# Decoding float64 weights: the sign bit by a narrowed copy on GpSimd or ScalarE, the second block's triangular solve on VectorE spread over the first block's Mish units, and the chain behind it moved beside the first expert

## The chip, the cores and the metric

One NeuronCore of one Trainium2 chip runs the whole kernel in one launch. The metric is the device time of the launch in microseconds (us). TensorE is called PE here, VectorE DVE, ScalarE ACT, GpSimd POOL, and the engine that issues the DMAs SP.

## The reference

A delta-rule attention feeds a dense layer with a Mish activation, which feeds a mixture of eight experts whose gates are balanced by eight Sinkhorn rounds. Cut to what is computed:

```python
for t in range(S):                      # q, k, v: [4, 8, 768, 48]
    y[:, :, t] = einsum(q_t, state)
    v_old = einsum(state, k_t)
    state = state + beta_t * outer(k_t, v_t - v_old)
x = y as [3072, 384]
h = x @ w_in                            # w_in [384, 2048]: float64
x = (h * tanh(softplus(h))) @ w_out     # w_out [2048, 384]: float64
P = exp(x @ w_gate), scaled eight times by rows and columns
out = sum over e of P[:, e] * (relu(x @ w1[e]) @ w2[e])   # 8 experts, 1024 wide
```

`w_in` and `w_out` come from numpy as float64, so the kernel gets their 64-bit words and has to make float32 values of them itself.

## The kernel before

The 768 positions are cut into six **blocks** (`c` = 0 to 5) of 128 positions, each with all 4 x 8 heads. For each block the delta rule needs the inverse of 32 x 32 triangles (the **solve**) and then a **chain** of small matrix products; its result, `x1`, is the input of the dense layer.

The solve: `lane_in_one` transposes `gx` into `lane`; `elim_ops` gives 60 operations (30 products into `t`, 30 sums into `lane`); `st_lane_out` transposes the result into `t` and `yd`; then `st_m1`, `st_place` and `st_m2` join the quarters with 128 and 128 matmuls of 32 x 32. The chain (`chain_list`) is z, w, s, y for two halves of the block, each stage a pair of tiles: matmuls into a bank called `psa`, and an eviction (`r`, `us`, `us`, `yd`). Block 0's solve and chain run in a **start** written out by hand.

After the start, `window(c)` places the work of the next block beside the matmuls of block c. Block 0 has 16 **Mish units** (marks s0 to s15), then marks f1 to f4, then 8 units of expert 0 (marks s16 to s23). A Mish unit f is: `m_first`, nine matmuls into `psh` (called gemm f below); Mish and a rounded copy `gh` on ACT; the rest `gl` on DVE (`m_c`); and `m_second`, nine matmuls into `x`. There are two `psh` banks, so gemm f+2 waits until `gl` f has read its bank. After the last unit, `x2_done` evicts `x`, which expert 0 reads. At the end of the block `st_x1` turns `yd` into the next block's `x1`. Blocks 2 to 5 have a Mish part of their own each, and only blocks 0 and 1 an expert part; a second phase with the other experts follows.

Each Mish unit of block 0 needs one **chunk** of 128 columns of `w_in` and 128 rows of `w_out`, made of 64-bit words in a tile of 128 x 1536 words of 32 bits (`bits`, `xr`, and from chunk 4 on four `kq` tiles in turn). Of each number the tile has a low and a high 32-bit word, so each operation works on 128 x 768 with a stride of two words. The decode is

- ACT (`begin_decode`): the high word, read as float32, times 2^-112, which moves the exponent's bias;
- DVE `tail`: low word shifted right by 29;
- DVE `shift`: low word = high word shifted left by 3, or low word;
- DVE `sign`: low word = sign bit of the high word, or low word;
- ACT rounds the float32 into a weight slot `w`, and DVE subtracts to get the rest (`convert`), after which SP fetches the chunk that reuses the tile.

Operations on an engine run in the order in which the program issues them, apart from what the framework moves up where nothing stands against it. Three queues set the order on DVE: `dq` holds decode steps, `eq` the solve's operations with a cost each, and `fill(us)` issues operations of `eq` at the end of a unit until their costs reach `us`. `PLACES[0]` says at which marks the next block's solve is finished (its first number), at which the sixteen chain stages stand (the list behind it), and from which mark on the solve after it is queued (its last number but one). In the list of marks 0 to 15 are s0 to s15, 16 to 19 are f1 to f4, and 20 to 27 are s16 to s23.

Of the kernel before, what the change touches and what calls it, by code (L numbers as in the profile page):

```python
# [10 lines left out]
F16 = mybir.dt.float16  # L11
I32 = mybir.dt.int32
AF = mybir.ActivationFunctionType
ALU = mybir.AluOpType
# [70 lines left out]
def delta_mish_sinkhorn_kernel(  # L85
# [94 lines left out]

    def queue_decode(i):

        if kind(i) != "wide":
            return
        b = bits(i).rearrange("p (n w) -> p n w", w=2)
        low, high = b[:, :, 0], b[:, :, 1]

        def tail():
            nc.vector.tensor_scalar(out=low, in0=low, scalar1=29, scalar2=None, op0=ALU.logical_shift_right)

        def shift():
            nc.vector.scalar_tensor_tensor(
                out=low, in0=high, scalar=3, in1=low, op0=ALU.logical_shift_left, op1=ALU.bitwise_or
            )

        def sign():
            nc.vector.scalar_tensor_tensor(
                out=low, in0=high, scalar=-0x80000000, in1=low, op0=ALU.bitwise_and, op1=ALU.bitwise_or
            )
            decoded[0] = i + 1  # L200

        dq.extend([(0.47, tail, i), (0.87, shift, i), (0.87, sign, i)])

    def begin_decode(i):
        high = bits(i).rearrange("p (n w) -> p n w", w=2)[:, :, 1].bitcast(F32)
        nc.scalar.activation(out=high, in_=high, func=AF.Copy, scale=2.0 ** -112)
        queue_decode(i)
        begun[0] = i + 1
# [28 lines left out]
    def flush_stores():  # L237

        while late_stores:
            late_stores.popleft()()  # L240

    def convert():
        i = ncvt[0]
        if kind(i) == "wide":
            while decoded[0] <= i:
                while not dq:
                    begin_decode(begun[0])
                dq.popleft()[1]()
        ncvt[0] += 1
        w = wslots[loads[i][2]]  # L250
        ch = loads[i][1]
        if kind(i) == "again":
            flush_stores()
            nc.sync.dma_start(out=w.bitcast(F32), in_=w_dram[ch])
            return
        if kind(i) == "wide":
            r = bits(i).rearrange("p (a b w) -> p a b w", a=2, w=2)[:, :, :, 0].bitcast(F32)
        else:
            r = raws.pop(i)
        nc.scalar.activation(out=w[:, 0], in_=r, func=AF.Copy)  # L260
# [516 lines left out]
    def o_store():  # L777

        u, half, t = todo.popleft()
        if t < 0:  # L780
            f, x, (n, d) = fin[u], slice(512 * half, 512 * half + 512), divmod(~t, KD)
            tt(out=f[:, d, x], in0=f[:, d, x], in1=f[:, 3 + 3 * n + d, x], op=ALU.add)
            return
            return True
        o_write(u, half, t, o_turn(u, half, t, (0, 1, 2)))
# [10 lines left out]
    if True:  # L796
# [277 lines left out]

        def elim_ops(c, eng=(nc.vector,)):
            ops = []
            for s in range(1, 31):
# [3 lines left out]
                def prod(s=s, n=n, slot=slot):  # L1081
                    slot[0] = t11.rearrange("p b i -> p (b i)")[:, 0:n * s].rearrange("p (n s) -> p n s", s=s)
                    eng[0].tensor_tensor(  # L1083
                        out=slot[0], in0=lane[:, s + 1:32, s:s + 1].to_broadcast([128, n, s]),
                        in1=lane[:, s:s + 1, 0:s].to_broadcast([128, n, s]), op=ALU.mult,
                    )

                def add(s=s, n=n, slot=slot):
                    eng[0].tensor_tensor(  # L1089
                        out=lane[:, s + 1:32, 0:s], in0=lane[:, s + 1:32, 0:s], in1=slot[0], op=ALU.add  # L1090
                    )
# [265 lines left out]
        with tc.manual_schedule():  # L1357
# [61 lines left out]
            for t in range(4):  # L1419
                run(*[lambda hf=hf: st_g(1, t, hf, False) for hf in range(2)])  # L1420
            for n in range(4):
                begin_decode(n)
# [9 lines left out]

            def elim1(n, eng):
                elim_eng[0] = eng
                for _ in range(min(n, len(ops1))):
                    ops1.popleft()[1]()

            m1a = m_run(st_m1(0, 0, (32,)))
            m1a[0]()
            st_place(0, 0, (0, 2))  # L1440
            dec(2)
            m1b, m2a = m_run(st_m1(0, 1, (32,)), st_m2(0, 0, (0,)))
# [9 lines left out]
            for p in wa:  # L1452
                p()
            dec(1)
            st_place(0, 1, (0, 1, 2, 3))
            m2b = m_run(st_m2(0, 1, (0,)))
            s0 = [st_s(0, t) for t in range(2)]
            m2b[0]()
            for t in range(2, 4):
                prep_v_act(0, t)  # L1460
            s0[0]()
            s0[1]()
            converts(1)
            z1 = [st_z(0, t) for t in range(2, 4)]
            z1[0]()
            gq[0]()
            z1[1]()
            gq[1]()
            run(*[lambda t=t: st_y(0, t) for t in range(2)])
            for n in range(4, 6):  # L1470
                fetch(n)
            for t in range(4):
                diag_left(1, t)
            in1 = [op for _, op in lane_in_one(1)]
            elim_eng = [nc.gpsimd]
            ops1 = deque(elim_ops(1, elim_eng))
            dec(2)
            wb = [st_w(0, t) for t in range(2, 4)]
# [5 lines left out]
            for n in range(6, 8):  # L1484
                fetch(n)
            decodes(2)
            converts(2)
            dec(2)
            x1h, x1l = [late_p.tile([128, KD, 512], F32R, tag=f"e{i}", name=f"x{i}") for i in range(2)]
# [7 lines left out]
            converts(3)  # L1497
            elim1(18, nc.gpsimd)
            decodes(4)
            converts(4)  # L1500
            elim_eng[0] = nc.vector
            wslots.append(late_p.tile([128, 2, 2, DM], F32R, tag="e2", name=f"w{NS1 - 1}"))
# [9 lines left out]
        def drain_decode():  # L1512
# [4 lines left out]
        PLACES = [  # L1517
            (11, two(14, 15, 17, 18, 19, 20, 21, 22), 16, [21, 22, 23, 24], two(23, 24, 25, 26), 18, 26, 26),
            (5, spread(8, 23, 1, 16), 1, [8, 9, 11, 13], spread(10, 19, 1, 8), 1, 27, 19),
# [4 lines left out]
        def window(c):  # L1524
# [53 lines left out]
        with tc.manual_schedule():  # L1578
            banks[:] = [0, [A1, A1]]
            for c in range(NBLK):  # L1580
# [36 lines left out]
                for f in range(U1 + (3 if c < NE0 else 2)):  # L1617
# [240 lines left out]
```

## Time and profile before

| what | value |
|---|---|
| median of 3 runs | 2230.39 us (2229.17 to 2235.85) |
| the profiled execution's own time | 2229.53 us |
| its span in the profile | 2227.7 us |
| PE busy, share of the span | 2165.4 us, 97% |
| DVE busy | 1394.4 us, 63% |
| ACT busy | 691.9 us, 31% |
| POOL busy | 673.6 us, 30% |

The span is what the trace covers; the profiled execution's time is 1.8 us more, and the median 0.9 us above that. A busy share is a mean over the whole span; the change touches the first 290 us of it, where the shares differ from the mean. The time at the start of an operation is counted from the span's start.

### The profile page before, as it was taken

The page shows a single profiled execution, that of the slowest core. Times are in us where ns is not written, and L with a number is a line of the kernel's source. Part 1 is how long each engine was busy: PE and PEld are TensorE (multiplying, and loading weights), DVE is VectorE, ACT ScalarE, POOL GpSimd, SP SyncE. Part 2 cuts the span into 40 slices and gives each one's busy share as a digit, 9 for nine tenths or more (in the row PEclk, how much of TensorE's full clock was granted, in tenths as well). Part 3 has the DMA queues.
Part 4 walks back from the last instruction along what each step waited for, and adds up shares of the span by engine and source line. Part 5 has one row for each costly group of instructions (what it writes and reads, how often), then busy time and mean ns, then how long its engine had stood idle before and what let it go on. Part 6 is the DMA issues. An engine that isn't in the chain of part 4 may idle for free.

```text
span 2227.7 us, 34746 instructions
## 1 busy us (share of the span) xinstructions
PE 2165.4 (97%) x14133; PEld 1792.0 (80%) x14133; DVE 1394.4 (63%) x2289; ACT 691.9 (31%) x1212; POOL 673.6 (30%) x528
## 2 busy tenths in 40 slices
PE   7889898999999999999999999999999999999999
PEld 6668787888888788888888888888888888888887
DVE  8894726473821276777776776666666666666665
ACT  6453332333324445233333322112212121211122
POOL 3504441435324656677878600000000000000000
PEclk7799999999999999999999999999999999999999
DMA  6576733544446446655555444444443454444441
GB/s 185 184 245 202 232 124 133 191 165 154 143 143 207 161 156 221 233 195 199 202 195 197 153 143 155 150 148 161 138 161 124 150 154 158 137 147 147 165 151 43
DMA packets 123648, 370.35 MB, mean 166 GB/s; under 512 B 9440, under 2 KB 51232, under 8 KB 123232
## 3 DMA queue, kind: packets, MB, share of 16 engines
q1 hardware_dynamic: 122912, 367.74, 48.3%
q8 instruction: 111, 1.82, 0.3%
q10 hardware_dynamic: 576, 0.39, 0.1%
q14 instruction: 49, 0.40, 0.1%
HBM read 274.15 MB, written 93.95 MB: 165 GB/s over the span
## 4 chain that ended last, share of the span: by engine, by line
PE 86%; DVE 8%; issue 2%; DMA 1%; POOL 1%; ACT 1%; SPq 0%; DVEq 0%; POOLq 0%; ACTq 0%
PE s L663 33%; PE b L596 31%; PE psh L300 7%; PE x L1310 6%; DVE t L1083 1%; DVE lane L1089 1%; PE y L324 1%; PE psa L1020 1%; DVE us L876 1%; PE psa L1168 1%; DVE lane L1053 1%; PE psa L1126 1%; PE psa L1141 1%; PE psa L1224 1%; PE psa L1190 1%
## 5 line engine op out<-in xcount | busy, mean ns | idle before, releaser
L596 PE MATMUL b<-gx,gw 128*128 128x512 f32 x3036 | 795.5, 390 | 0.1
L603 DVE TENSOR_TENSOR gt<-b,gt 128x512 f32<-128x512 f32 x644 | 436.0, 689 | 460.8 <-PE b L596 429.5
L596 PEld LDWEIGHTS b<-gx,gw 128*128 128x128 f32 x3036 | 568.5, 188 | 118.6 <-ACT gt L605 0.9
L663 PE MATMUL s<-gh,gw 128*128 128x512 f32 x2208 | 622.7, 390 | 0.6 <-DVE gy L706 0.4
L638 ACT ACTIVATE gh<-gt 128x512 fp32r<-128x512 f32 x368 | 232.8, 633 | 933.5 <-DVE gt L632 926.1
L663 PEld LDWEIGHTS s<-gh,gw 128*128 128x128 f32 x2208 | 413.6, 188 | 87.0 <-DVE gy L706 0.8
L663 PE MATMUL s<-gl,gw 128*128 128x512 f32 x1104 | 326.8, 390 | 0.0
L632 DVE SCALAR_TENSOR_TENSOR gt<-gt,gp 128x512 f32<-128x512 f32 x336 | 277.0, 825 | 4.5
L300 PE MATMUL psh<-x,w 128*128 128x512 f32 x1008 | 262.0, 405 | 11.8 <-DVE gl L1299 10.1
L663 PEld LDWEIGHTS s<-gl,gw 128*128 128x128 f32 x1104 | 206.8, 188 | 42.8
L300 PEld LDWEIGHTS psh<-x,w 128*128 128x128 f32 x1008 | 188.2, 192 | 59.8 <-DVE gl L1299 9.5
L641 POOL TENSOR_TENSOR gl<-gt,gh 128x512 fp32r<-128x512 f32 x128 | 186.3, 1462 | 77.4 <-ACT gh L638 72.3
L641 DVE TENSOR_TENSOR gl<-gt,gh 128x512 fp32r<-128x512 f32 x240 | 164.5, 686 | 37.0 <-ACT gh L638 36.8
L1299 POOL TENSOR_TENSOR gl<-x,gh 128x512 fp32r<-128x512 f32 x80 | 103.0, 1288 | 256.1 <-ACT gh L1297 238.5
L536 POOL TENSOR_TENSOR gx<-gxr,gx 128x768 fp32r<-128x768 f32 x18 | 33.3, 1847 | 407.0 <-ACT gx L535 407.0
L1310 PE MATMUL x<-gh,w 128*128 128x512 f32 x576 | 155.3, 406 | 0.0
L467 POOL TENSOR_TENSOR gw<-gr,gw 128x640 fp32r<-128x640 f32 x70 | 117.5, 1680 | 68.2 <-ACT gw L477 66.4
L1310 PEld LDWEIGHTS x<-gh,w 128*128 128x128 f32 x576 | 109.4, 194 | 24.0 <-issue 1.4
L1291 ACT ACTIVATE x<-psh 128x512 f32<-128x512 f32 x80 | 47.7, 596 | 132.3 <-PE psh L300 123.3
L1310 PE MATMUL x<-gl,w 128*128 128x512 f32 x288 | 82.8, 396 | 2.3 <-POOL gl L1299 2.3
L467 POOL TENSOR_TENSOR gw<-raw,gw 128x384 fp32r<-128x384 f32 x70 | 73.3, 1068 | 7.3 <-ACT gw L499 7.3
L984 POOL TENSOR_TENSOR kq<-kq,mask_sb 64x256 f32<-64x256 f32 (+1 forms) x72 | 58.6, 814 | 55.0 <-ACT kq L979 51.2
(203 smaller groups left out, 1984.8 us busy)
## 6 DMA issues: line engine op xcount, KB each, us to landing
gw<-wg SPq DMA_DIRECT2D x57, 1280.0 KB, 8.1
w<-wd SPq DMA_DIRECT2D x88, 768.0 KB, 4.4
gw<-wg SPq DMA_DIRECT2D x57, 768.0 KB, 5.1
wg<-gw SPq DMA_DIRECT2D x29, 1280.0 KB, 6.0
wg<-gw SPq DMA_DIRECT2D x29, 768.0 KB, 5.3
wd<-w SPq DMA_DIRECT2D x24, 768.0 KB, 5.7
gr<-in_w_dram SPq DMA_DIRECT2D x35, 384.0 KB, 3.2
raw<-in_w_dram SPq DMA_DIRECT2D x35, 384.0 KB, 3.8
```

Of the source, the lines that this page charges most:

```text
L300: mm(ps, lhsT=wi(u, pw, kc), rhs=(xh, xl)[px][:, kc, :], start=(n == 0), stop=(n == 3 * KD - 1))
L467: nc.gpsimd.tensor_tensor(out=w[:, 1, lo:hi], in0=r, in1=w[:, 0, lo:hi].bitcast(F32), op=ALU.subtract)
L596: mm(ps, lhsT=w[:, pw, i * 128:i * 128 + 128], rhs=x[:, px, j, :], start=(n == 0), stop=(n == last))
L603: add = lambda o, i: nc.vector.tensor_tensor(out=t[:, o], in0=ps, in1=t[:, i], op=ALU.add)
L632: nc.vector.scalar_tensor_tensor(out=t, in0=t, scalar=0.0, in1=pbs[u, e][:, o:o + 512], op0=ALU.max, op1=ALU.mult)
L638: nc.scalar.activation(out=h, in_=t, func=AF.Copy)
L641: return lambda: eng.tensor_tensor(out=l, in0=t, in1=h.bitcast(F32), op=ALU.subtract)
L663: mm(o[k], lhsT=w[:, pw, at:at + 128], rhs=hids[s, z][ph], start=(start and new and n == 0), stop=(end and not new and n == 2))
L984: nc.gpsimd.tensor_tensor(out=o, in0=o, in1=mask_sb[p, None, :].to_broadcast([64, hs.stop - hs.start, CH]), op=ALU.mult)
L1291: nc.scalar.activation(out=mi_x[u % 2], in_=hps.pop(u), func=AF.Mish)
L1299: eng.tensor_tensor(out=l, in0=p, in1=h.bitcast(F32), op=ALU.subtract)
L1310: mm(x2ps[c][k], lhsT=wo(u, pw, k * 128, k * 128 + 128), rhs=(h, l)[pg], start=(f == 0 and n == 0), stop=(f == U1 - 1 and n == 2))
```

## The change

The sign is no longer merged by a logical operation on DVE. The scaled high word is tiny as float32, so that a copy of it into float16 gives plus or minus zero: 16 bits of which only the first, the sign, can be set. These 16 bits are written over the upper half of the low word, after `tail` has put its three bits into the lower half; `shift` then merges everything. For chunks 4 to 15 the copy is on POOL (its rows say CAST). For chunks 0 to 3 it is on ACT, and `tail` too is on ACT, as a scaled copy of the upper 16 bits. In the start, the decode of chunks 2 and 3 begins later, the rounding (`rounded`) is issued apart from the subtraction, and 18 operations of block 1's solve that POOL did there are left to DVE in the Mish units, with `fill(1.4)` for `fill(1.2)`. Block 1's solve ends at mark 17 (f2) where it was 11, and its chain stands at marks 20 to 27, two stages each.

```diff
+        value, sign = high.bitcast(F32), halves(i, F16)[:, :, 1]
+        nc.scalar.activation(out=value, in_=value, func=AF.Copy, scale=2.0 ** -112)
         def tail():
             nc.vector.tensor_scalar(out=low, in0=low, scalar1=29, scalar2=None, op0=ALU.logical_shift_right)
+            nc.gpsimd.tensor_copy(out=sign, in_=value)
...
-        def sign():
-            nc.vector.scalar_tensor_tensor(
-                out=low, in0=high, scalar=-0x80000000, in1=low, op0=ALU.bitwise_and, op1=ALU.bitwise_or
-            )
             decoded[0] = i + 1
-        dq.extend([(0.47, tail, i), (0.87, shift, i), (0.87, sign, i)])
...
+        if i < 4:
+            h = halves(i, U16)
+            nc.scalar.activation(out=h[:, :, 0], in_=h[:, :, 1], func=AF.Copy, scale=2.0 ** -13, bias=-0.49994)
+            nc.scalar.activation(out=sign, in_=value, func=AF.Copy)
+        else:
+            dq.append((0.57, tail, i))
+        dq.append((0.97, shift, i))
...
-            elim1(18, nc.gpsimd)
...
-            (11, two(14, 15, 17, 18, 19, 20, 21, 22), 16, [21, 22, 23, 24], two(23, 24, 25, 26), 18, 26, 26),
+            (17, two(20, 21, 22, 23, 24, 25, 26, 27), 16, [21, 22, 24, 25], two(23, 24, 25, 26), 18, 26, 27),
...
-                rest["s3"].append(lambda: eq.extend(ops1))
+                rest["s1"].append(lambda: eq.extend(ops1))
...
+                    if not c and len(dq) == 2:
+                        dq.popleft()[1]()
...
-                    fill(1.2 if not c else 3.2 if c >= NE0 and f > 8 else 2.0)
+                    fill(1.4 if not c else 3.2 if c >= NE0 and f > 8 else 2.0)
```

**DVE, one Mish unit of block 0.** `kq_142` is the tile of the chunk being decoded, `w` the weight slot of the chunk before it, `lane` and `t_167` are the solve. Before:

```order
L1299 TENSOR_TENSOR gl<-psh,gh 128x512
L1083 TENSOR_TENSOR t_167<-lane 128x210
L1089 TENSOR_TENSOR lane<-lane,t_167 128x21x10
L1083 TENSOR_TENSOR t_167<-lane 128x220
L189 TENSOR_SCALAR kq_142<-kq_142 128x768
L192 SCALAR_TENSOR_TENSOR kq_142<-kq_142 128x768
L197 SCALAR_TENSOR_TENSOR kq_142<-kq_142 128x768
L262 TENSOR_TENSOR w_1167<-kq_141,w_1167 128x768
```

The same place in the changed kernel:

```order
L1308 TENSOR_TENSOR gl<-psh,gh 128x512
L193 TENSOR_SCALAR kq_142<-kq_142 128x768
L1098 TENSOR_TENSOR lane<-lane,t_167 128x25x6
L1092 TENSOR_TENSOR t_167<-lane 128x168
L1098 TENSOR_TENSOR lane<-lane,t_167 128x24x7
L1092 TENSOR_TENSOR t_167<-lane 128x184
L197 SCALAR_TENSOR_TENSOR kq_142<-kq_142 128x768
L272 TENSOR_TENSOR w_1149<-kq_141,w_1149 128x768
```

One of the three wide decode operations is gone, the shift by 29 stands ahead of the solve's operations, and four of these stand in a unit where there were three.

**POOL, the same units.** `vt_151` is block 1's scaled v, `kq_144` its masked keys; both products were in the start before. Changed kernel:

```order
L194 CAST kq_142<-kq_142 128x768
L973 TENSOR_TENSOR vt_151<-vt_151,ne_159 128x384
L194 CAST kq_143<-kq_143 128x768
L993 TENSOR_TENSOR kq_144<-kq_144,mask_sb 64x512
L194 CAST kq_140<-kq_140 128x768
L973 TENSOR_TENSOR vt_151<-vt_151,ne_159 128x384
L993 TENSOR_TENSOR kq_144<-kq_144,mask_sb 64x512
```

POOL now has one CAST a unit, and behind some of them the products that it had done before the first unit.

**PE, behind the last Mish unit.** `psa<-t_167,gx_153` and `psa<-yd,mb` join the quarters of block 1's solve, `psa<-us_162,kq_144` is the chain's first stage. Changed kernel:

```order
L1319 MATMUL x_1245<-gl,w_92 128x512
L1319 MATMUL x_1246<-gl,w_92 128x512
L1319 MATMUL x_1247<-gl,w_92 128x512
L1135 MATMUL psa<-t_167,gx_153 32x32 x64
L1150 MATMUL psa<-yd,mb_176 32x32 x32
L1150 MATMUL psa<-yd,mb_177 32x32 x32
L1177 MATMUL psa<-us_162,kq_144 64x48
```

Before, the first of these joins stood between the two halves of a Mish unit, three units ahead of the last:

```order
L300 MATMUL psh<-x_1107,w_89 128x512 x2
L300 MATMUL psh<-x_1108,w_89 128x512
L1126 MATMUL psa<-t_167,gx_153 32x32 x64
L1310 MATMUL x_1255<-gh,w_93 128x512
L1310 MATMUL x_1256<-gh,w_93 128x512
```

They now stand behind all matmuls of the Mish part, and ahead of the first of expert 0.

## Rows read from the trace of the kernel before

**Rows 1.** The page's first lines: the span, PE's busy time.

```profile
span 2227.7 us, 34746 instructions
PE 2165.4 (97%) x14133; PEld 1792.0 (80%) x14133; DVE 1394.4 (63%) x2289; ACT 691.9 (31%) x1212; POOL 673.6 (30%) x528
```

**Rows 2.** PE's waits from 80 to 300 us: total us, times, longest.

```profile
PE psh L300 <- DVE gl L1299: 10.1, 10, 4.4
PE psa L1126 <- DVE t L1098: 10.0, 2, 5.5
```

**Rows 3.** DVE in the start, in order of time: start us, us, operation.

```profile
59.46 1.81 DVE L262 TENSOR_TENSOR w<-bits,w 128x768 fp32r<-128x768 f32 x1 [1.29 <-ACT w L260]
...
64.99 1.18 DVE L189 TENSOR_SCALAR bits<-bits 128x768 int32<-128x768 int32 x1
66.20 1.91 DVE L192 SCALAR_TENSOR_TENSOR bits<-bits 128x768 int32<-128x768 int32 x1
...
79.28 1.89 DVE L876 TENSOR_TENSOR x<-psa,x 128x512 fp32r<-128x512 f32 x3
```

**Rows 4.** DVE in one Mish unit of block 0, in order of time.

```profile
112.13 0.56 DVE L189 TENSOR_SCALAR kq<-kq 128x768 int32<-128x768 int32 x1
112.72 0.96 DVE L192 SCALAR_TENSOR_TENSOR kq<-kq 128x768 int32<-128x768 int32 x1
113.71 0.96 DVE L197 SCALAR_TENSOR_TENSOR kq<-kq 128x768 int32<-128x768 int32 x1
114.59 0.95 DVE L262 TENSOR_TENSOR w<-kq,w 128x768 fp32r<-128x768 f32 x1
115.46 0.68 DVE L1299 TENSOR_TENSOR gl<-psh,gh 128x512 fp32r<-128x512 f32 x1
116.06 0.40 DVE L1089 TENSOR_TENSOR lane<-lane,t 128x238 f32<-128x238 f32 x1
...
117.26 0.56 DVE L189 TENSOR_SCALAR kq<-kq 128x768 int32<-128x768 int32 x1
```

**Rows 5.** POOL, in order of time.

```profile
49.66 2.40 POOL L964 TENSOR_TENSOR vt<-vt,ne 128x384 f32<-128x384 f32 x3 [19.48 <-DVE ne L947]
...
62.35 1.26 POOL L984 TENSOR_TENSOR kq<-kq,mask_sb 64x512 f32<-64x512 f32 x1
...
84.08 2.26 POOL L1065 MEMSET gx<- 32x1024 f32 x2 [12.18 <-DVE lane L1070]
...
163.66 1.81 POOL L262 TENSOR_TENSOR w<-raw,w 128x768 fp32r<-128x768 f32 x1 [62.89 <-ACT w L260]
...
188.48 5.44 POOL L925 TENSOR_TENSOR ne<-ss,half_sb 128x32 f32<-128x32 f32 x1 [15.36 <-DVE ss L909]
...
269.01 1.28 POOL L1299 TENSOR_TENSOR gl<-x,gh 128x512 fp32r<-128x512 f32 x1 [2.35 <-ACT gh L1297]
```

**Rows 6.** DVE, an operation of the solve beside POOL's last row above.

```profile
268.82 0.32 DVE L1083 TENSOR_TENSOR t<-lane 128x150 f32<-128x150 f32 x1
269.18 1.30 DVE L1089 TENSOR_TENSOR lane<-lane,t 128x150 f32<-128x150 f32 x1
```

**Rows 7.** PE in block 0, in order of time.

```profile
101.25 2.21 PE L300 MATMUL psh<-x,w 128*128 128x512 f32 x9
...
163.92 0.25 PE L1168 MATMUL psa<-us,kq 48*64 48x48 f32 x1
...
165.91 2.33 PE L300 MATMUL psh<-x,w 128*128 128x512 f32 x9
...
178.56 0.24 PE L1208 MATMUL psa<-us,kt 64*48 64x48 f32 x1
...
180.14 1.66 PE L1310 MATMUL x<-gh,w 128*128 128x512 f32 x6
...
182.41 0.26 PE L1224 MATMUL psa<-us,kq 112*64 112x48 f32 x1
...
199.77 2.33 PE L300 MATMUL psh<-x,w 128*128 128x512 f32 x9
```

**Rows 8.** PE in block 1, in order of time.

```profile
275.40 3.62 PE L1126 MATMUL psa<-t,gx 32*32 32x32 f32 x128 [4.53 <-DVE t L1098]
```

More of the change, by code (lines that the diff above doesn't have):

```diff
@@ L12 @@
 I32 = mybir.dt.int32
+U16 = mybir.dt.uint16
 AF = mybir.ActivationFunctionType
@@ L179, in fetch, with halves, begin_decode @@
         raws[i] = r
-    def queue_decode(i):
-        if kind(i) != "wide":
-            return
+    def halves(i, dt):
+        return bits(i).bitcast(dt).rearrange("p (n w) -> p n w", w=4)
+    def begin_decode(i):
         b = bits(i).rearrange("p (n w) -> p n w", w=2)
         low, high = b[:, :, 0], b[:, :, 1]
+        value, sign = high.bitcast(F32), halves(i, F16)[:, :, 1]
+        nc.scalar.activation(out=value, in_=value, func=AF.Copy, scale=2.0 ** -112)
         def tail():
             nc.vector.tensor_scalar(out=low, in0=low, scalar1=29, scalar2=None, op0=ALU.logical_shift_right)
+            nc.gpsimd.tensor_copy(out=sign, in_=value)
         def shift():
@@ L194, in shift @@
             )
-        def sign():
-            nc.vector.scalar_tensor_tensor(
-                out=low, in0=high, scalar=-0x80000000, in1=low, op0=ALU.bitwise_and, op1=ALU.bitwise_or
-            )
             decoded[0] = i + 1
-        dq.extend([(0.47, tail, i), (0.87, shift, i), (0.87, sign, i)])
[L204 to L207, printed above, removed]
+        if i < 4:
[5 more added lines that the diff above has]
+        dq.append((0.97, shift, i))
         begun[0] = i + 1
@@ L240, in flush_stores, with rounded @@
             late_stores.popleft()()
+    reads = {}
+    def rounded(i):
+        if i not in reads:
+            if kind(i) == "wide":
+                r = bits(i).rearrange("p (a b w) -> p a b w", a=2, w=2)[:, :, :, 0].bitcast(F32)
+            else:
+                r = raws.pop(i)
+            nc.scalar.activation(out=wslots[loads[i][2]][:, 0], in_=r, func=AF.Copy)
+            reads[i] = r
+        return reads[i]
     def convert():
@@ L255, in convert @@
             return
[L256 to L260, printed above, removed]
+        r = rounded(i)
         eng = nc.vector if kind(i) == "wide" else nc.gpsimd
@@ L783, in o_store @@
             return
-            return True
         o_write(u, half, t, o_turn(u, half, t, (0, 1, 2)))
@@ L1073, in lane_in_one, with elim_ops @@
             ]
-        def elim_ops(c, eng=(nc.vector,)):
+        def elim_ops(c):
             ops = []
@@ L1082, in prod @@
                     slot[0] = t11.rearrange("p b i -> p (b i)")[:, 0:n * s].rearrange("p (n s) -> p n s", s=s)
-                    eng[0].tensor_tensor(
+                    nc.vector.tensor_tensor(
                         out=slot[0], in0=lane[:, s + 1:32, s:s + 1].to_broadcast([128, n, s]),
@@ L1088, in add @@
                 def add(s=s, n=n, slot=slot):
-                    eng[0].tensor_tensor(
+                    nc.vector.tensor_tensor(
                         out=lane[:, s + 1:32, 0:s], in0=lane[:, s + 1:32, 0:s], in1=slot[0], op=ALU.add
@@ L1420, in delta_mish_sinkhorn_kernel @@
                 run(*[lambda hf=hf: st_g(1, t, hf, False) for hf in range(2)])
-            for n in range(4):
+            for n in range(2):
                 begin_decode(n)
@@ L1431, in dec @@
                     dq.popleft()[1]()
[L1433 to L1436, printed above, removed]
             m1a = m_run(st_m1(0, 0, (32,)))
@@ L1440, in delta_mish_sinkhorn_kernel @@
             st_place(0, 0, (0, 2))
-            dec(2)
+            dec(1)
             m1b, m2a = m_run(st_m1(0, 1, (32,)), st_m2(0, 0, (0,)))
@@ L1453, in delta_mish_sinkhorn_kernel @@
                 p()
-            dec(1)
+            rounded(0)
             st_place(0, 1, (0, 1, 2, 3))
+            converts(1)
             m2b = m_run(st_m2(0, 1, (0,)))
@@ L1460, in delta_mish_sinkhorn_kernel @@
                 prep_v_act(0, t)
+            for n in range(2, 4):
+                begin_decode(n)
             s0[0]()
             s0[1]()
-            converts(1)
             z1 = [st_z(0, t) for t in range(2, 4)]
@@ L1468, in delta_mish_sinkhorn_kernel @@
             gq[1]()
+            dec(1)
             run(*[lambda t=t: st_y(0, t) for t in range(2)])
@@ L1471, in delta_mish_sinkhorn_kernel @@
                 fetch(n)
+            rounded(1)
             for t in range(4):
@@ L1474, in delta_mish_sinkhorn_kernel @@
             in1 = [op for _, op in lane_in_one(1)]
-            elim_eng = [nc.gpsimd]
-            ops1 = deque(elim_ops(1, elim_eng))
-            dec(2)
+            ops1 = deque(elim_ops(1))
             wb = [st_w(0, t) for t in range(2, 4)]
@@ L1485, in delta_mish_sinkhorn_kernel @@
                 fetch(n)
-            decodes(2)
             converts(2)
-            dec(2)
+            dec(1)
             x1h, x1l = [late_p.tile([128, KD, 512], F32R, tag=f"e{i}", name=f"x{i}") for i in range(2)]
@@ L1497, in delta_mish_sinkhorn_kernel @@
             converts(3)
-            elim1(18, nc.gpsimd)
             decodes(4)
             converts(4)
-            elim_eng[0] = nc.vector
             wslots.append(late_p.tile([128, 2, 2, DM], F32R, tag="e2", name=f"w{NS1 - 1}"))
```

## Prediction

> **What bounds the kernel now.** I read the page's first lines, then PE's waits over the stretch that the change touches, then DVE's and POOL's operations in order of time, and last PE's marks there. PE is busy 97% of the span [rows 1], so over the whole kernel it is PE that sets the end; about 62 us are idle. The waits between 80 and 300 us tell what ends some of that idleness: ten times a gemm waits for DVE's `gl` to release its bank (10.1 us, the longest 4.4), and twice the quarters of a triangle solve wait for DVE's last transposes (10.0 us) [rows 2]. One of these two is block 2's, 4.53 us at 275.40 [rows 8].
>
> In the Mish units of block 0 DVE sets the pace. From one `tail` to the next are 117.26 - 112.13 = 5.13 us, without a gap: tail 0.59 (start to start), shift 0.99, sign 0.88, subtraction 0.87, `gl` 0.60, and three operations of the solve at 0.40, 1.20 [rows 4]. PE's part of a unit is nine matmuls into `psh` and nine into `x`, 18 at about 0.246 (2.21 for nine, [rows 7]), some 4.4. So PE stands idle 0.7 us a unit, and an operation that leaves DVE there is worth its length until DVE's unit falls under 4.4.
>
> **The change part by part.** The sum goes against the profiled execution's own time, 2229.53; the median is 0.86 above that.
>
> *Start.* DVE's work ahead of the end of the `x1` evictions (79.28 + 1.89 = 81.17) is one nearly unbroken row. The subtraction of chunk 0 moves up into the place of a sign that is gone, so that at 59.46 its 1.81 and the 1.29 of waiting for ACT's rounding go; the tail of 1.18 at 64.99 goes to ACT; the shift of 1.91 beside POOL's masks should take the 0.96 of an undisturbed one, since POOL has left that place [rows 3 and 4]. Together 1.29 + 1.81 + 1.18 + 0.95 = 5.23. ACT gets two more copies per chunk in this stretch, and PE's stages between these operations take their own time, so some comes back as waiting. Bounds: 2.6 (half) to 5.2; I take **-4.0**.
>
> *First units, up to gemm 4.* From 81.17 to gemm 4 at 101.25 are 20.1 us [rows 3 and 7]. Four signs of about 1.05 go (0.96 undisturbed, [rows 4]), 4.2; so does what waits for POOL's 18 solve operations, which lies in the 4.4 us wait [rows 2]. Solve operations start on DVE at mark s1 instead, eleven in this stretch by `fill(1.4)`, about 3.1 us since the first ones are short. I get 16 us, **-4.25**. Bounds -1.1 (the wait is only taken over by the solve) to -5.5.
>
> *Ten units, gemm 4 to gemm 14.* Before: 165.91 - 101.25 = 64.66 [rows 7]; this holds DVE's units, the end of the solve, its quarters on PE with a wait, and a z stage of 1.99. After, DVE alone makes 0.59 + 0.99 + 0.87 + 0.60 = 3.05 a unit, and the 40 or so operations of the solve that remain 16.0: 46.5 us, which is 4.65 a unit, still above PE's 4.4. What these 46.5 leave out is POOL, which in this stretch did next to nothing before and now has ten CASTs of 128 x 768, four products for `vt` and six masks for `kq`. No row shows a CAST on POOL. A MEMSET of 32 x 1024, which reads nothing, took 1.13; at its rate 768 elements are 0.85; the subtraction with two inputs of 128 x 768 took 1.81 [rows 5]. I take 0.85, as the CAST has one input. What it does to DVE is bounded below by nothing, as a MEMSET may leave DVE alone, and above by its whole length, 1.81. The nearest row is the last of POOL's group: while POOL's product of 128 x 512 ran for 1.28 us, a DVE operation of the solve took 1.30, and the same size just ahead of it 0.32 [rows 5 and 6]. So 0.98 was lost, three quarters of POOL's 1.28. About a sixth of a DVE unit is operations that read one tensor of SBUF (`gl` reads PSUM), so I charge two thirds of POOL's length: 0.55 a CAST, 0.52 for a `vt` (0.80, a third of 2.40), 0.82 for a `kq` (1.26) [rows 5]. 10 x 0.55 + 4 x 0.52 + 6 x 0.82 = 12.5. With this the stretch is 59.0 us, **-5.65**. Bounds: 46.5 (-18.2), and 59.0 plus ten times what a whole 1.81 has over 0.55, 71.6 (+6.9).
>
> Here a page of the Trainium skill bears on the row. SBUF — State Buffer, section "Who interferes with whom", says that DVE's second input and GpSimd's reads go through one shared pair of ports, held for a whole instruction, and that a DVE operation with one SBUF input is outside this. The row agrees: the operation that stood beside POOL took as long as POOL did, 1.30 against 1.28. By that rule the CAST, which reads SBUF, takes from DVE what it saves; it speaks against this change. The GPSIMD Engine Reference, section "Engine selection", has one-input work on GpSimd at roughly line rate; as an estimate from it a CAST would be shorter than my 0.85 and the sum about 1.4 us lower. No run so far shows a CAST, and the sum goes by the rows.
>
> *Gemm 14 to the end of the last second half.* Before 182.41 - 165.91 = 16.5, with two chain stages in it (1.58, from 178.56 to 180.14, is one [rows 7]; the other is a 64-matmul stage of z's size, 1.99). Without them 12.9; DVE is still behind at the last units, for which I add 1.2: **-2.4** (bounds -3.6 to 0).
>
> *From there to the end of the first gemm of expert 0.* Before 199.77 + 2.33 - 182.41 = 19.7 [rows 7]. This gap is a sequence: evictions, norm, POOL's power of 5.44 [rows 5], products, with PE's work of chain stages beside it. Now the stages are gone from it, and in come the quarters of block 1's solve (the like in block 2 is 3.62, [rows 8]), whose transposes stand on DVE behind the evictions of `x1`. The power starts later by what these hold DVE. I take **+2.65**; bounds 0 (all of it fits under POOL's 5.44) to +4.5.
>
> *Chain beside expert 0.* Five stages that lay in the Mish units and the gap now stand at the marks of expert 0, where PE has no idle time to give. At z's 165.91 - 163.92 = 1.99 and s's 1.58 [rows 7] that is 1.58 + 3 x 1.99 + 1.58 = 9.1: **+9.15**, with little uncertainty, as PE's work is the same wherever it stands; what differs is only whether it stands in idle time.
>
> *Block 2's solve.* It is queued one mark later, 27 for 26: 11 operations of the previous window's end, 3.8 us, are then done after the block changes, and PE already waits 4.53 for it [rows 8]. Less 0.4 of waiting for POOL and 0.9 since the evictions ahead of it come earlier: **+2.5** (bounds 0 to +3.8).
>
> Sum: -4.0 - 4.25 - 5.65 - 2.4 + 2.65 + 9.15 + 2.5 = **-2.0**, which makes 2227.5. Sixteen us are won ahead of expert 0 and fourteen given back behind it.
>
> **The rivals.** *A: POOL costs DVE nothing.* For it: the one POOL operation whose cost to DVE is seen has two inputs, and a CAST has one. Against it is that row itself, the 1.30 of [rows 6], and it would have to hold for `vt` and `kq` too, which have two. Then the 46.5 holds but for PE, which doesn't fall under 4.4 a unit, so nearly all of the 12.5 goes: 2227.5 - 12.5 = 2215, and 2213 with the start's upper bound.
>
> *B, on the slow side: a CAST is as slow as POOL's two-input operation and holds DVE as long.* If strided 16-bit writes make it 1.81 [rows 5] and it costs 1.4 of DVE, then each unit is 0.85 longer; with the eleventh behind the stretch +9.4: 2237. Eleven times what a CAST costs over my 0.55 is added to the sum: from 0.73 on the kernel is slower than before, from about 1.4 on by over 0.3%. For it: every POOL operation in [rows 5] is at half of DVE's speed or less. Against: it reads one input, and runs partly beside `gl` and `shift`.
>
> *C: the chain stalls beside expert 0.* A stage there waits for the eviction of the one before, and expert 0 follows late, with PE's clock lower after such gaps; with 0.6 a stage for eight stages +5: 2232.5. Against it: marks are one gemm apart.
>
> *D: the start gives little.* DVE's row in the start is only as long as PE and ACT let it; with the lower bounds there (-2.6 and -1.1) the time is 2232.
>
> **How the numbers follow.** A measurement tells a change from none at about 0.3%, 6.7 us: 2223.7 and 2237.1. The forecast (two thirds of POOL's length) has a chance of 0.45 and its own range 2222 to 2233, A 0.27, B 0.14, C and D 0.07 each. Faster by over 0.3%: A's 0.27 and 0.11 from the lower part of the forecast, 0.38. Slower by over 0.3%: 0.08 from B (about half of it lies over 2237.1), 0.05 from the upper part of the forecast and 0.03 from C and D, 0.16. The rest, 0.46, is within 0.3%. For 8 in 10 the range reaches from 2213, where A ends, to 2238, which holds B's middle.
>
> **What would show it.** Right: DVE's unit at 4.65 plus about one us, CASTs of 0.7 to 1.0, operations of the solve that take over 0.9 where a CAST runs and 0.4 elsewhere; the `x1` evictions end near 77, the last second half near 166, and block 2's wait is 7 us or more. Wrong: operations of the solve at 0.4 beside a CAST (A); CASTs of 1.8 (B); the same matmuls of expert 0 over a longer time than before plus 9 (C); evictions that end at 79 or later (D). The sum fails most easily in the ten units, where one number, the cost of a POOL operation to DVE, is multiplied by twenty, and in the gap behind the Mish part, where three engines take turns.

## The result and the profile after

The changed kernel takes 2244.35 us (median of 4 runs, 2243.1 to 2245.8) against 2229.78 before: a ratio of 1.0061, 95% interval 1.0040 to 1.0082. It is slower by about 14 us (13.6 by the ratio, 14.6 by the medians), where 2227.5 was forecast and 2238 was the range's end. The profiled execution's span went from 2227.7 to 2241.3, +13.6 us.

The page's first lines after, against [rows 1]:

```profile
span 2241.3 us, 34762 instructions
PE 2168.3 (97%) x14133; PEld 1793.9 (80%) x14133; DVE 1405.4 (63%) x2287; ACT 706.1 (32%) x1220; POOL 681.2 (30%) x522
```

PE's busy time grew by 3 us; the other 10.7 us are PE waiting. PE's waits from 80 to 300 us after (total us, times, longest), against [rows 2]:

```profile
PE psh L310 <- DVE gl L1308: 22.1, 12, 3.8
PE psa L1135 <- DVE t L1107: 12.8, 2, 8.1
```

By the forecast, which brings DVE's unit nearer to PE's 4.4, the wait for `gl` was to shrink; it has doubled. DVE shows why. One Mish unit of block 0 after (start, us), against [rows 4]:

```profile
101.84 0.55 DVE L193 TENSOR_SCALAR kq<-kq 128x768 int32<-128x768 int32 x1
102.30 0.34 DVE L1098 TENSOR_TENSOR lane<-lane,t 128x184 f32<-128x184 f32 x1
102.68 1.80 DVE L1092 TENSOR_TENSOR t<-lane 128x198 f32<-128x198 f32 x1
104.51 0.37 DVE L1098 TENSOR_TENSOR lane<-lane,t 128x198 f32<-128x198 f32 x1
104.92 0.38 DVE L1092 TENSOR_TENSOR t<-lane 128x210 f32<-128x210 f32 x1
105.21 0.95 DVE L197 SCALAR_TENSOR_TENSOR kq<-kq 128x768 int32<-128x768 int32 x1
106.08 0.95 DVE L272 TENSOR_TENSOR w<-kq,w 128x768 fp32r<-128x768 f32 x1
106.95 0.68 DVE L1308 TENSOR_TENSOR gl<-psh,gh 128x512 fp32r<-128x512 f32 x1
107.55 0.55 DVE L193 TENSOR_SCALAR kq<-kq 128x768 int32<-128x768 int32 x1
```

And POOL at the same place, against [rows 5]:

```profile
102.59 1.90 POOL L194 CAST kq<-kq 128x768 f16<-128x768 f32 x1 [3.59 <-ACT kq L190]
108.22 1.96 POOL L194 CAST kq<-kq 128x768 f16<-128x768 f32 x1 [3.72 <-DVE kq L193]
110.00 0.86 POOL L973 TENSOR_TENSOR vt<-vt,ne 128x384 f32<-128x384 f32 x1
```

The unit is 107.55 - 101.84 = 5.71 us without a gap, longer than the 5.13 of before, with the sign's 0.88 gone and one solve operation of some 0.4 more. DVE is busy 64.0 of the 65.1 us from gemm 4 to gemm 14, so that it sets the pace there. The second solve operation takes 1.80 where its neighbours take 0.34 to 0.38. It ends at 104.48, and the CAST at 104.49: DVE had the operation in hand and got through only when POOL was done. The CAST is 1.90 to 1.96 us, more than twice the 0.85 that I took.

Where an operation of DVE is not held is seen at the end of the Mish part, beside POOL's subtraction for expert 0:

```profile
167.53 2.57 POOL L272 TENSOR_TENSOR w<-raw,w 128x768 fp32r<-128x768 f32 x1
```

```profile
167.47 0.95 DVE L272 TENSOR_TENSOR w<-kq,w 128x768 fp32r<-128x768 f32 x1
168.34 0.68 DVE L1308 TENSOR_TENSOR gl<-psh,gh 128x512 fp32r<-128x512 f32 x1
168.94 1.23 DVE L1092 TENSOR_TENSOR t<-lane 128x58 f32<-128x58 f32 x1
170.21 0.22 DVE L1098 TENSOR_TENSOR lane<-lane,t 128x58 f32<-128x58 f32 x1
```

`gl`, with one input in PSUM, keeps its 0.68 in the middle of POOL's operation; the solve's 0.2 behind it lasts until POOL ends at 170.1. The hold goes the other way too: POOL's 2.57 is 0.76 more than the 1.81 of a like subtraction in [rows 5], and DVE's own subtraction, with two SBUF inputs, had started 0.06 us ahead of it and ran for 0.95.

Where POOL reads nothing, no hold is seen. Two MEMSETs, and DVE's shift beside them, which has both inputs in SBUF and keeps its 0.95:

```profile
81.56 1.93 POOL L1074 MEMSET gx<- 32x1024 f32 x2
```

```profile
82.35 0.95 DVE L197 SCALAR_TENSOR_TENSOR bits<-bits 128x768 int32<-128x768 int32 x1
```

PE's marks after, against [rows 7, 8]:

```profile
95.80 2.34 PE L310 MATMUL psh<-x,w 128*128 128x512 f32 x9 [1.30 <-DVE gl L1308]
...
160.88 2.37 PE L310 MATMUL psh<-x,w 128*128 128x512 f32 x9 [1.54 <-DVE gl L1308]
...
179.03 0.84 PE L1319 MATMUL x<-gl,w 128*128 128x512 f32 x3
...
200.75 2.34 PE L310 MATMUL psh<-x,w 128*128 128x512 f32 x9
...
254.37 2.31 PE L310 MATMUL psh<-x,w 128*128 128x512 f32 x9
...
288.43 3.62 PE L1135 MATMUL psa<-t,gx 32*32 32x32 f32 x128 [8.06 <-DVE t L1107]
```

The end of the `x1` evictions after, 77.58 + 1.89 = 79.47, and block 1's first gemm before:

```profile
77.58 1.89 DVE L885 TENSOR_TENSOR x<-psa,x 128x512 fp32r<-128x512 f32 x3 [1.14 <-ACT x L1243]
```

```profile
244.48 2.57 PE L300 MATMUL psh<-x,w 128*128 128x512 f32 x9
```

Step by step (the last second half ended at 182.5 before):

| step | forecast | measured | from |
|---|---|---|---|
| start, to the end of the `x1` evictions | -4.0 | -1.7 | 81.17 to 79.47 |
| to gemm 4 | -4.25 | -3.75 | 20.08 to 16.33 |
| gemm 4 to gemm 14 | -5.65 | +0.4 | 64.66 to 65.08 |
| gemm 14 to the last second half's end | -2.4 | +2.4 | 16.6 to 19.0 |
| to the end of expert 0's first gemm | +2.65 | +3.6 | 19.6 to 23.2 |
| expert 0, with five chain stages more | +9.15 | +8.9 | 42.4 to 51.3 |
| block 2's solve, from block 1's first gemm to its quarters | +2.5 | +3.1 | 30.92 to 34.06; the wait in it 4.53 to 8.06 |
| rest | 0 | +0.6 | 13.6 less the others |

Of the miss of 15.6 us, 10.9 lie in the third and fourth rows and 2.3 in the first.

### The profile page after: what moved, and what is told of

Same layout as the page of the kernel before. It is cut to its first block, busy times and chain, and to the rows that moved or that the text cites. A ratio compares the mean times of both kernels' runs of the same rounds, so it can differ in the third digit from the quotient of the medians.

```text
span 2241.3 us, 34762 instructions
## 1 busy us (share of the span) xinstructions
PE 2168.3 (97%) x14133; PEld 1793.9 (80%) x14133; DVE 1405.4 (63%) x2287; ACT 706.1 (32%) x1220; POOL 681.2 (30%) x522
## 4 chain that ended last, share of the span: by engine, by line
PE 88%; DVE 7%; ACT 2%; issue 1%; DMA 1%; POOL 0%; SPq 0%; DVEq 0%; ACTq 0%; POOLq 0%
PE s L673 33%; PE b L606 31%; PE psh L310 9%; PE x L1319 7%; PE y L334 2%; DVE t L1092 1%; PE psa L1029 1%; DVE lane L1098 1%; PE psa L1177 1%; PE psa L1199 1%; PE psa L1233 1%; PE psa L1150 1%; PE psa L1135 1%; DVE us L885 1%; DVE lane L1062 1%
## 5 line engine op out<-in xcount | busy, mean ns | idle before, releaser
L310 PE MATMUL psh<-x,w 128*128 128x512 f32 x1008 | 268.3, 413 | 23.5 <-DVE gl L1308 22.1
L1092 DVE TENSOR_TENSOR t<-lane 128x30 f32<-128x30 f32 (+9 forms) x180 | 92.0, 511 | 5.8
```

What stands on the lines that cost most here:

```text
L310: mm(ps, lhsT=wi(u, pw, kc), rhs=(xh, xl)[px][:, kc, :], start=(n == 0), stop=(n == 3 * KD - 1))
L1092: nc.vector.tensor_tensor(out=slot[0], in0=lane[:, s + 1:32, s:s + 1].to_broadcast([128, n, s]), in1=lane[:, s:s + 1, 0:s].to_broadcast([1 ...
```

## The experiments

The theory: **a POOL operation that reads SBUF stops a DVE operation with two SBUF inputs until POOL is done**, the CAST is long, and the units carry both it and the products that POOL did in the start before. The rival: four solve operations a unit and PE's lower clock set the units' length. Medians below are each with its ratio to the kernel before, run beside it; between medians of different batches the kernel before itself differs by up to 1.8 us.

**The sign of chunks 4 to 15 on ACT.**

```diff
-            nc.gpsimd.tensor_copy(out=sign, in_=value)
+            nc.scalar.activation(out=sign, in_=value, func=AF.Copy)
```

> The sign copies of chunks 4 to 15 are on ACT, POOL has no CAST, and its vt and kq products go back into the start by themselves. Theory (a POOL operation that reads SBUF stops one solve operation of DVE until it ends; 1.4 to 1.5 us for a CAST of 1.93): no solve operation of DVE over 0.5 us in the Mish units, about 16 us of the CASTs and 6 of the products gone from DVE there, a unit near PE's 4.4 to 4.7, the last second half near 162 instead of 179.9, some 3 us lost in the start, time 2226 to 2230. Rival (the units are long because of four solve operations a unit and PE's lower clock, not of POOL): units stay at 5.8 to 6.7, time 2240 or more.

2235.31 us, ratio 1.0021 (1.0012 to 1.0031), 9 us faster than the changed kernel. No solve operation in the units is over 0.41: the hold is gone with POOL's work, as the theory has it. But the units are 5.8 us still, a length that the rival named, and the forecast of 2226 to 2230 missed. It is not four solve operations that make them so long, since DVE waits some 1.3 us in each, and not PE's clock: from gemm 4 to gemm 14 it was granted at 1.00 of full speed here (the upper of its two levels throughout), for a mean of 0.90 in the changed kernel. ACT and DVE wait for each other:

```profile
107.24 0.61 ACT L1298 ACTIVATE psh<-psh 128x512 f32<-128x512 f32 x1
107.88 0.60 ACT L1306 ACTIVATE gh<-psh 128x512 fp32r<-128x512 f32 x1
109.70 1.96 ACT L194 ACTIVATE kq<-kq 128x768 f16<-128x768 f32 x1 [1.23 <-DVE kq L193]
111.40 0.94 ACT L252 ACTIVATE w<-kq 128x768 fp32r<-128x768 f32 x1
112.25 0.91 ACT L190 ACTIVATE kq<-kq 128x768 f32<-128x768 f32 x1
113.05 0.58 ACT L1298 ACTIVATE psh<-psh 128x512 f32<-128x512 f32 x1
```

ACT waits for DVE's `tail`, the next Mish stands behind the sign, the rounding and the scaling, and DVE's `gl` and `tail` wait for that Mish. The copy into 16 bits takes 1.96, the scaling of as many numbers into 32 bits 0.91. So the narrow copy is slow on ACT as on POOL.

**All of the decode but the shift on ACT.**

```diff
-        if i < 4:
+        if i < 16:
```

> Chunks 4 to 15 are decoded as chunks 0 to 3: sign and tail both on ACT. Theory: as the run with the sign alone on ACT, and DVE loses the tail's 0.55 a unit too, so that PE's 4.4 is the limit; 2223 to 2229, unless ACT's three operations in a row delay Mish, which would show as waits of PE for gl with DVE idle. Rival: 2238 or more.

2247.01 us, ratio 1.0069 (1.0054 to 1.0084). A miss: with two narrow copies of 1.9 to 2.0 ACT is busy 61.9 of the 64 us from 102 to 166, and PE waits 14.2 us there for `gl` while DVE is busy only 39.9. ACT has become the bound; the run says nothing about POOL.

**The sign of chunks 4 to 15 on DVE, as before.** `merge` is the old logical operation followed by `shift`.

```diff
-            nc.gpsimd.tensor_copy(out=sign, in_=value)
...
-        dq.append((0.97, shift, i))
+        dq.append((0.97, shift if i < 4 else merge, i))
```

> The sign of chunks 4 to 15 is merged on DVE by the logical operation of before (0.88 us a unit), everything else as in the changed kernel; POOL has no CAST. Theory: 0.88 comes for 1.45, and the products of vt and kq leave the units: 12 x 0.57 + 6 - 3 = 10 us faster than the changed kernel, 2233 to 2237. Rival (POOL costs DVE nothing): the units are 0.88 longer each, 2250 to 2255.

2232.70 us, ratio 1.0009 (1.0000 to 1.0018): 11.7 us faster than the changed kernel with 0.88 us more of DVE's own work in each unit, and 0.3 below the range expected. The rival would have it slower. Gemm 4 to gemm 14 takes 52.5 us for 65.1.

**Each CAST twice.**

```diff
             nc.gpsimd.tensor_copy(out=sign, in_=value)
+            nc.gpsimd.tensor_copy(out=sign, in_=value)
```

> Each CAST on POOL is issued twice. Theory: the second stops another solve operation, 1.5 us a unit, the ten units from gemm 4 to gemm 14 go from 65.1 to 79 or more; 2258 to 2264. Rival (POOL costs DVE nothing, or only shift waits for the sign): the second lies in POOL's idle time, 2243 to 2247.

2263.61 us, ratio 1.0145 (1.0130 to 1.0160), 19.3 us over the changed kernel. Gemm 4 to gemm 14 takes 80.0: 1.49 us for each second CAST. On DVE two operations a unit are now held:

```profile
108.69 1.80 DVE L1093 TENSOR_TENSOR t<-lane 128x198 f32<-128x198 f32 x1
110.52 0.37 DVE L1099 TENSOR_TENSOR lane<-lane,t 128x198 f32<-128x198 f32 x1
110.92 1.72 DVE L1093 TENSOR_TENSOR t<-lane 128x210 f32<-128x210 f32 x1
```

**A 32-bit copy behind each CAST**, to see what makes the CAST long.

```diff
             nc.gpsimd.tensor_copy(out=sign, in_=value)
+            nc.gpsimd.tensor_copy(out=value, in_=value)
```

> Behind each CAST POOL copies the same high words onto themselves, 32 bits to 32 bits, same stride; the rest is the changed kernel. What makes the CAST 1.93 us: Theory (the narrow, strided write: ACT's copy into 16 bits took 1.96 where its 32-bit one takes 0.93): the added copy takes 0.9 to 1.1 us, stops one more solve operation for 0.5 to 0.7, time 2249 to 2254. Rival (POOL needs 1.9 for 768 elements of any kind): the added copy takes as long as the CAST, and the time is that of the doubled CAST, 2263.

2251.73 us, ratio 1.0091 (1.0071 to 1.0111), 7.4 us over the changed kernel. POOL:

```profile
110.60 1.95 POOL L194 CAST kq<-kq 128x768 f16<-128x768 f32 x1 [3.17 <-DVE kq L193]
112.61 1.07 POOL L195 COPY kq<-kq 128x768 f32<-128x768 f32 x1
```

In the units the same numbers at the same stride take 0.91 to 1.12 with 32 bits written and 1.90 to 1.99 with 16. With one input and 32 bits written POOL comes near my 0.85; the narrow copy takes twice that. The CAST changes the type as well, and on POOL no run took type and width apart. On ACT it is not the type: the `tail` of chunks 0 to 3, in the changed kernel, copies 16 bits to 16 bits of the same type.

```profile
38.67 1.90 ACT L204 ACTIVATE bits<-bits 128x768 uint16<-128x768 uint16 x1
```

POOL's 32-bit copy holds its solve operation too (0.94 for 0.40 at 113.00).

**Block 2's solve queued at mark 26 again**, on the kernel with the sign on DVE. The products that fill block 2's matrix are then not all ahead of its solve: the last is evicted into it at 234.28, behind the solve's first transposition at 232.15. The solve so works on wrong numbers, with the same amount of work; the run prices the place and is no kernel to use.

```diff
-            (17, two(20, 21, 22, 23, 24, 25, 26, 27), 16, [21, 22, 24, 25], two(23, 24, 25, 26), 18, 26, 27),
+            (17, two(20, 21, 22, 23, 24, 25, 26, 27), 16, [21, 22, 24, 25], two(23, 24, 25, 26), 18, 26, 26),
```

> The kernel with the sign on DVE, and block 2's solve queued at mark 26 again, as before the change, instead of 27. Theory (the eleven operations left over make PE's wait for the solve in block 1 8.0 us instead of 4.5): the wait falls to about 4.5, 3 to 3.5 us less than with the sign on DVE alone, 2229 to 2230. Rival (DVE is late there for another reason, the evictions at the block's end): the wait stays at 7 to 8, 2232 to 2233.

2229.92 us, ratio 0.9994 (0.9984 to 1.0003), 2.8 less, and the wait is 3.3 us for 8.0:

```profile
277.68 3.41 PE L1140 MATMUL psa<-t,gx 32*32 32x32 f32 x128 [3.33 <-DVE t L1112]
```

So the later queueing is that wait. With the chain where it stands now it is needed: at marks 23 to 26 the two chain stages come first, and the products of block 2 behind them.

**The places alone**, on the kernel before.

```diff
-            (11, two(14, 15, 17, 18, 19, 20, 21, 22), 16, [21, 22, 23, 24], two(23, 24, 25, 26), 18, 26, 26),
+            (17, two(20, 21, 22, 23, 24, 25, 26, 27), 16, [21, 22, 24, 25], two(23, 24, 25, 26), 18, 26, 27),
```

> The kernel before with one row of numbers changed: block 1's solve ends at mark 17, its chain stands at 20 to 27, block 2's solve is queued at 27. Decode, start and POOL's share of the solve are those of before. Theory (the rearrangement by itself wins in the Mish units about what it gives back behind them): the last second half ends 13 to 16 us earlier, at 167 to 170; 3 us come back in the gap, 9 beside expert 0 and 3.5 in block 1; 2229 to 2234. Rival (the chain beside expert 0 costs more than its matmuls, or the gap more than 4): 2236 or more. Second rival: the rearrangement is what gains, and the decode what loses: 2224 or less.

2233.02 us, ratio 1.0012 (1.0003 to 1.0022). The last second half ends at 167.6 for 182.5, and expert 0's first gemm at 193.0 for 202.1. Block 1's first gemm starts at 244.30, against 244.48: all is given back beside expert 0. Then the wait for block 2's solve is 8.16 for 4.53. The terms of +9.15 and +2.5 stand without any change to the decode.

**The hybrid**: the new start with chunks 0 to 3 on ACT, and all else as before (places, POOL's 18 solve operations, sign on DVE).

```diff
-            ops1 = deque(elim_ops(1))
+            elim_eng = [nc.gpsimd]
+            ops1 = deque(elim_ops(1, elim_eng))
...
+            for _ in range(18):
+                ops1.popleft()[1]()
...
-                rest["s1"].append(lambda: eq.extend(ops1))
+                rest["s3"].append(lambda: eq.extend(ops1))
```

> The new start (chunks 0 to 3 decoded on ACT), and all else as before: the sign of chunks 4 to 15 on DVE, 18 operations of block 1's solve on POOL in the start, the old places. Theory (of the change only the start gains, 1.7 us at the end of the x1 evictions, for ACT's narrow copies of 1.95 make PE wait 3.9 for ACT there): 2227 to 2230. Rival (the start gains as forecast, 4 us or more): 2226 or less.

2225.96 us, ratio 0.9973 (0.9963 to 0.9983): faster than both kernels. The time is the rival's, the place is not: the evictions of `x1` end at 79.2, 1.9 earlier, about what the theory says of the start, and 2.6 us more come behind it (gemm 5 starts at 101.42 for 105.99), with a DVE unit of 4.96 for 5.13 since `tail` is issued ahead of the solve.

**The hybrid with the CAST on POOL** for chunks 6 to 15.

```diff
+            if i > 5:
+                nc.gpsimd.tensor_copy(out=sign, in_=value)
...
-        dq.append((0.97, shift if i < 4 else merge, i))
+        dq.append((0.97, merge if i in (4, 5) else shift, i))
```

> The hybrid (new start, old places, sign on DVE from chunk 4 on) with one thing changed: the sign of chunks 6 to 15 is a CAST on POOL, as in the changed kernel. Theory (a CAST of 1.95 costs DVE 1.45 and saves 0.88; POOL's vt and kq products stand behind CASTs and move from the start into the units, 0.5 and 0.5 to 0.9 each where DVE still has solve operations): 5.7 plus 2 to 5 us more than the hybrid's 2226.0, 2233 to 2237. Rival (the CAST's price in the changed kernel came of its places: four solve operations a unit): 2226 to 2229.

2236.61 us, ratio 1.0031 (1.0020 to 1.0042), 10.6 us over the hybrid by the medians and 12.9 by the ratios: ten CASTs cost with the old places about what twelve cost with the new (11.7).

**The hybrid with chunks 0 to 3 decoded by DVE.**

```diff
-        if i < 4:
-            h = halves(i, U16)
...
-        else:
-            dq.append((0.57, tail, i))
-        dq.append((0.97, shift if i < 4 else merge, i))
+        dq.append((0.57, tail, i))
+        dq.append((0.97, merge, i))
...
-            dec(1)
+            dec(2)
```

> The hybrid with chunks 0 to 3 decoded by DVE's tail, sign and shift again; the moved subtraction and rounding of the new start stay, ACT has no narrow copy at all. Theory (ACT's copies take 1.51 us per chunk off DVE's row in the start and give 3.3 us back as PE's wait for ACT): the wait of 3.9 for ACT's mb is under 1, DVE's row about 3 us longer behind it, 2226 to 2229. Rival (the gain of the hybrid is all of ACT's copies): 2229 to 2231. Second rival (it is all of the moved subtraction, and ACT's copies only cost): 2224 or less.

2226.65 us, ratio 0.9983 (0.9973 to 0.9992), the hybrid within a microsecond, as the theory has it. PE's wait for ACT's `mb` in the start, first in the changed kernel:

```profile
47.65 0.31 PE L1150 MATMUL psa<-yd,mb 32*32 32x32 f32 x2 [3.92 <-ACT mb L1123]
```

then here:

```profile
44.33 0.31 PE L1150 MATMUL psa<-yd,mb 32*32 32x32 f32 x2 [0.61 <-ACT mb L1123]
```

ACT's copies take work from DVE and give it back as PE's wait; on balance they are worth nothing. What gains is among what the two kernels share: the moved subtraction, the later start of chunks 2 and 3, and `tail` issued ahead of the solve's operations. No run takes these apart.

**The hybrid with chunks 0 and 1 by DVE, 2 and 3 by ACT.**

```diff
-        if i < 4:
+        if 2 <= i < 4:
...
-        dq.append((0.97, shift if i < 4 else merge, i))
+        dq.append((0.97, shift if 2 <= i < 4 else merge, i))
...
-            dec(1)
+            dec(2)
```

> The hybrid with chunks 0 and 1 decoded by DVE's tail, sign and shift, chunks 2 and 3 on ACT. Theory (the wait of 3.9 us for ACT comes of the two narrow copies each of chunks 0 and 1, which stand ahead of ACT's copy of mb): the wait is under 1, DVE gets 3.0 us more in its row, half of it in waits; the x1 evictions end 1 to 2 us earlier, 2224 to 2226. Rival (DVE's row alone sets the start): 2227 to 2229.

2224.54 us, ratio 0.9977 (0.9967 to 0.9986). The wait for `mb` is gone, the evictions end at 78.04, as expected. Its interval and the hybrid's overlap, so that the two can't be told apart by time.

**The changed kernel with block 1's products in the start.**

```diff
                 mask_g(1, t, nc.gpsimd)
+            for t in range(4):
+                prep_v(1, t)
+                mask_p(1, t)
...
-                for t in range(4):
-                    rest[f"s{2 * t + 3}"].append(lambda t=t: prep_v(1, t))
-                for i in range(8):
-                    rest[MARKS[i + 8]].append(lambda t=i // 2, w=1 + i % 2: mask_p(1, t, (w,)))
```

> The changed kernel with block 1's four vt products and eight kq masks issued on POOL in the start, ahead of the CASTs, where they ran before the change; the CASTs stay in the units. Theory (of some 12.5 us that POOL costs the ten units against the sign on DVE, about 7 are these products and 5.7 the CASTs; a vt stops DVE 0.5 us, a kq 0.5 to 0.9): gemm 4 to gemm 14 about 58 us for 65.1, up to 2 us lost in the start, 2237 to 2240. Rival (the CASTs alone hold DVE, the products lie in the same hold): 2243 to 2246.

2234.70 us, ratio 1.0020 (1.0010 to 1.0031): 9.6 us faster than the changed kernel, more than expected. Gemm 4 to gemm 14 is 57.1 us. DVE's solve operations (line, count, busy us, mean ns) from each kernel's gemm 4 to its gemm 14 price the holds: the changed kernel, then this one, then that with the sign on DVE.

```profile
L1092 DVE TENSOR_TENSOR t<-lane 128x168 f32<-128x168 f32 (+10 forms) x20 | 24.1, 1203 | 0.7
L1098 DVE TENSOR_TENSOR lane<-lane,t 128x150 f32<-128x150 f32 (+10 forms) x21 | 13.0, 621 | 0.3
```

```profile
L1092 DVE TENSOR_TENSOR t<-lane 128x168 f32<-128x168 f32 (+10 forms) x20 | 20.3, 1015 | 0.7
L1098 DVE TENSOR_TENSOR lane<-lane,t 128x150 f32<-128x150 f32 (+10 forms) x21 | 9.1, 431 | 0.3
```

```profile
L1103 DVE TENSOR_TENSOR lane<-lane,t 128x150 f32<-128x150 f32 (+10 forms) x21 | 7.7, 368 | 0.3
L1097 DVE TENSOR_TENSOR t<-lane 128x168 f32<-128x168 f32 (+10 forms) x20 | 7.5, 374 | 0.7
```

Together 37.1, 29.4 and 15.2 us for the same 41 operations. The ten CASTs hold DVE for 29.4 - 15.2 = 14.2 us there, the products for 37.1 - 29.4 = 7.7.

## Why the prediction was wrong

**The ten units, the step that failed.** The mechanism was named and placed rightly: POOL's reads hold DVE. Its size was not. I charged 12.5 us for POOL in "gemm 4 to gemm 14"; the solve's rows give 21.9, CASTs 14.2 for 5.5 (1.42 each for the 0.55 that I charged) and products 7.7 for 7.0. The stretch missed by 6.0 and not by these 9.4, since the rest of DVE's row took 65.1 - 21.9 = 43.2 where I had 46.5: an error the other way that hid a third of the first. The length was off most: I took 0.85 for a CAST from a MEMSET's rate, and it took 1.93. The share was off less: the CAST starts right behind `tail`, and what DVE does then are solve operations, all with two SBUF inputs, so that 1.80 for 0.37, a loss of 1.43, is three quarters of the CAST where I charged two thirds. (The "sixth of a DVE unit" behind the two thirds is nearer to a quarter by [rows 4], 0.59 + 0.60 of 5.13, and none of it stood beside a CAST.) I had this as rival B, with 1.4 a CAST and 2237, and gave it 0.14; its time still lacks what the last units and the start lost. What I had set against it (the CAST reads one input) counts inputs, and the CAST is long where it writes 16 bits: 1.95 against 1.07 for the 32-bit copy at the same stride.

The rule of the Trainium skill (SBUF — State Buffer, "Who interferes with whom") held in the rows shown, for CAST and copy with one input as for products with two, and for `gl`, which is outside it and kept its 0.68. It spoke against the change, and its price hangs on how long GpSimd takes, which I had wrong. From the one-input line rate of the Trainium skill (GPSIMD Engine Reference, "Engine selection") I had estimated less than 0.85; the 32-bit copy, at 0.91 to 1.12, is a little above that and the CAST, at 1.90 to 1.98, more than twice, and the measurement decides.

**The last units.** -2.4 forecast, +2.4 measured. I had left POOL out of this step. Its masks and the subtractions for expert 0 stand there beside the end of the solve, which before was long done; four of the last solve operations take 1.2 to 3.0 us each, and gemm 15 waits 3.78 us. With the sign on DVE it waits 3.80: this loss comes with the later solve and not with the CAST.

**The start.** -4.0 forecast, -1.7 measured, below the bound of 2.6. "ACT gets two more copies per chunk" was priced as part of what comes back; the four narrow copies of chunks 0 and 1 take 1.90 to 1.95 each ahead of ACT's `mb`, and PE waits 3.9 for it. That is not the whole of it: with all four chunks decoded by DVE the wait is gone and the evictions end at 79.1 all the same, and with chunks 2 and 3 on ACT at 78.0. My "nearly unbroken row" also passed over a wait of 2.50 us for ACT's rounding at 76.82. The wait of 1.29 ahead of the moved subtraction did go; what the move alone is worth, no run shows.

**What held.** The first units (-3.75), the chain beside expert 0 (+8.9 for +9.15), the gap and block 2's solve, within a microsecond each. The chain is right for its reason: PE is busy through all of the 51.3 us. The first units are in part luck, since a CAST that I had not charged there made a solve operation of 0.29 last 1.66 (at 91.06), while the mean granted clock of PE, which no term names, was 1.00 of full speed for 0.83 before. In the gap it was 0.71 for 0.83. Rival C, stages that stall beside expert 0, did not come true; A is refuted by every hold above; D was right for the start and not for the first units.

With sign on DVE or CAST and with old or new arrangement (the new one leaves POOL's 18 operations to DVE), four kernels with the new start take 2226.0, 2236.6, 2232.7 and 2244.35: the CAST adds 10.6 and 11.7, the arrangement 6.7 and 7.7 (the places alone added 2.4 to the kernel before), and the new start's order takes 4.6 off. Ratios in place of medians move each of these by up to 2.3 us, and the first pair has ten CASTs for twelve; neither changes a sign. So the change consists of one part that gains and two that lose, and what the forecast of -2.0 lacked most is the CAST's price, with POOL's work beside the last units second.

## What to carry to other kernels

Before work moves from a busy VectorE to an idle GpSimd, look at what VectorE does in that very place: an operation with both inputs in SBUF waited here for the end of each GpSimd operation that reads SBUF, and the move pays only if GpSimd's operation is shorter than what is saved plus what VectorE gets done beside it (the held operation itself, and such as read PSUM). Take the duration of an operation from a row with the same output type and stride; here 16 bits written for 32 doubled it on two engines. An arrangement that empties one stage must be summed to the next stage that PE bounds: here 9 us won ahead of expert 0 were paid there in full.

## What the runs showed of the hardware

A copy of 128 x 768 numbers out of every second 32-bit word takes 0.91 to 1.12 us on POOL in the units and about 0.9 on ACT with a 32-bit output, and 1.9 to 2.0 on either with a 16-bit output into one half of each word. A held DVE operation is shown as one long operation (1.80 for 0.37), not as a wait. Beside the ten CASTs from gemm 4 to gemm 14 its end is POOL's within 0.08 us, beside a product of POOL it comes up to 0.26 later; at 163.22 in the changed kernel one of 0.25 lasted 3.00, across two POOL operations that followed each other without a gap. POOL is held in turn: where the CAST was issued twice, the second started 0.05 us behind a solve operation of 0.37 and took 2.09 (at 110.57). An operation with one SBUF input is not free of POOL either: `tail` takes 0.73 and 0.88 beside POOL's solve operations in the hybrid (at 89.37 and 94.15), and 0.55 in the units; POOL's operations there vary too, from 0.45 to 1.11 for nearly the same size. No run took this apart.
